# Linear attention's output product from f16 halves on two column groups of TensorE, and the output weights' forms made in one pass

## Chip, cores and metric

The kernel runs on one core of a Trainium2 chip. The metric is the device time of one execution in microseconds. A profile of one execution comes with it; its span runs from the first instruction to the last and is a little shorter than the device time.

The engines are named as in the profile: PE is TensorE's matrix multiplication and PEld its loading of weights, DVE is VectorE, ACT is ScalarE, POOL is GpSimd, and SP is SyncE, which here issues all transfers.

## What is computed

Two attention layers on separate inputs of 2048 tokens by 1024 features, 32 heads of 32 each, are computed and put side by side in a result of 2048 by 2048. Layer A is a softmax attention within four segments of 512 tokens with a compressive memory that is carried from segment to segment. Layer B is a linear attention with learned features, and the change lies in its second half and in A's output weights:

```python
q, k, v = qkv[0], qkv[1], qkv[2]
pq = jnp.einsum("bhsd,hdf->bhsf", q, w_phi)
pk = jnp.einsum("bhsd,hdf->bhsf", k, w_phi)
phi_q = jnp.concatenate([_softmax(pq, axis=-1), _softmax(-pq, axis=-1)], axis=-1)
phi_k = jnp.concatenate([_softmax(pk, axis=-1), _softmax(-pk, axis=-1)], axis=-1)
kv = jnp.einsum("bhsf,bhsd->bhfd", phi_k, v)
z  = jnp.einsum("bhsf->bhf", phi_k)
num = jnp.einsum("bhqf,bhfd->bhqd", phi_q, kv)
den = jnp.einsum("bhqf,bhf->bhq", phi_q, z)[..., None] + 1e-6
o = num / den
```

The result of each layer is then multiplied by its output weights `wo`, a matrix of 1024 by 1024.

## The kernel before

The inputs are f32, and most products are made from f16 halves. A number is scaled and split into a high half and a low half (what the high half left over); a product is then three matmuls, high by high, high by low and low by high, which add up in one bank of PSUM. `halves` (L377) does the split on ACT (high, L387) and DVE (low, L389); `split` (L345) does the same with f32r parts, a form of f32 that TensorE multiplies in one pass (L347 on ACT, L350 on DVE). `product` (L353, its matmuls at L360) runs the three matmuls over the depth. `strassen` (L544, matmuls at L552) computes a product of 2 by 2 blocks with seven block products; the sums of blocks that this needs are called forms, and `forms` (L451) makes them by a plan of steps (`XPLAN`, `WPLAN`): a subtraction of blocks on POOL (L459), then the halves. In its other mode, which takes blocks that are scaled already, the high half is a plain ACT copy (L466) and the low half a POOL subtraction (L467).

The program has four stages. First comes layer A's attention, head group by head group; layer B's weights are prepared beside it. Then come B's keys and values, eight pairs of row blocks of 128 tokens (L1217): projections by `strassen`, features by `expo` (L1102: maximum and minimum, two differences, the exponential on ACT, the sums r at L1125 and their reciprocal at L1128), the scaling on POOL (L1229), halves of the features (L1259, L1262), and the matmuls of features with values (L1269). DVE adds their results to `kva`, 64 by 64 numbers for each pair of heads of which only the two diagonal 32 by 32 blocks count; an addition for each half of the columns multiplies with `svm`, a scale made at L505 that is zero outside the own block (L1278 and L1281). The lower halves of the values are made at L1155, and Strassen's sums on DVE at L562. The keys' sums go to `za`.

The third stage is B's queries and output, 16 row blocks (L1387), and here the change lies. For each of two halves of the heads: features from `expo` (tile `e`, 16 heads by 64 features, five buffers); POOL multiplies them with the keys' sums `zb` into a tile `ez` that has one buffer, in two parts (L1418); DVE sums that to the denominators (L1420 to L1428); POOL scales `e` with the result (L1430). Then in two quarters, each for four pairs of heads: four transposes on PE (L1436); `split` to f32r parts `pt` (L347, L350); twelve matmuls with the keys' and values' sums `kls` as weights (L1446), 64 output rows for a pair of heads; and the eviction to the f16 halves `ot` by `halves`, for the first and the second pairs' outputs apart (L387, L389 on tiles of 64 rows by 256). A batch below means the twelve matmuls of one quarter; there are 16 x 2 x 2 = 64. `project` (L1318) multiplies `ot` with B's output weights (L360, output `misc`) and ACT scales the result (L1323). Between the row blocks, `weights` (L1357) makes the halves of A's output weights' seven forms: four blocks of columns, each read twice, three forms on the first reading and four on the second, subtractions on POOL (L1371), halves on ACT and DVE. The fourth stage is A's output product (L1459 on), by Strassen's method, with matmuls at L1498.

The order of the work is written by a planner, `Graph.run` (L148). Every `op` has an engine, an assumed duration and a priority, in most cases the number of its row block; the planner walks through time and gives each engine the ready operation of the lowest priority. What comes out is a fixed order for each engine, in which the engine then works, one instruction behind the other. So a changed duration or dependency changes the order of other work too. PSUM has eight banks, and the kind `pv`, into which the product goes, may hold one of them at a time (L77).

## Time and profile before

| what | value |
|---|---|
| median of 3 runs | 1818.51 us (1817.17 to 1818.78) |
| the profiled execution: device time | 1821.83 us |
| its span | 1819.5 us |
| instructions | 39261 |
| mean granted TensorE clock | 0.987 |
| bytes read and written in HBM | 149.64 and 85.00 MB |

In a row of the groups stand the line, the engine, the operation, what it writes and reads (buffer numbers left out), shapes, the count, the busy time in us with the mean ns of one, and the idle time of the engine before them with what ended it. A matmul's mean is its whole length; matmuls are pipelined, so the time that one takes from PE is the step from its start to the next one's start. In a row of waits stand who waited, for whom, the sum in us, how often, and the longest. In the order of time a row is a start, a length, an engine with its instruction, and how many were merged.

### The profile page before, as it was taken

To read this page: it belongs to the slowest core of one execution; us is meant where nothing else is said; L and a number is where in the kernel's file an instruction comes from. 1 tells how busy PE (TensorE), PEld (TensorE's weight loads), DVE (VectorE), ACT (ScalarE), POOL (GpSimd) and SP (SyncE) were. 2 spreads that over 40 slices of the span, in tenths; PEclk is the share of its full clock that TensorE was granted. 3 is DMA by queue.
4 is the path that set the end of the run, shared out by engine and by line. 5 is a ranking of instruction groups with operands and counts; after the bars stand their busy time and mean duration, and the time that the engine had idled before them with its cause. 6 is when DMAs were issued, how large, how long until landed. Compare 5 with 4: busy or idle time off the path is not lost. (4 is left out here: it accounts for less than half of the span.)

```text
span 1819.5 us, 39261 instructions
## 1 busy us (share of the span) xinstructions
PE 1747.2 (96%) x14712; PEld 1072.7 (59%) x14712; DVE 1503.4 (83%) x3523; ACT 1172.2 (64%) x2185; POOL 903.3 (50%) x1117
## 2 busy tenths in 40 slices
PE   8999998999999999999989999998999999999999
PEld 5767676677677766777544444444555555555444
DVE  6989989898777887888878999979998889887541
ACT  6896986877777877688756565546655455545341
POOL 6445454555757677678654444534444545431000
PEclk8999999999999999999989999999999999999999
DMA  6546554574545454574484343275323224334321
GB/s 202 168 141 197 138 173 137 170 216 148 149 115 146 132 171 124 164 213 118 141 274 144 139 156 134 89 265 222 111 64 104 83 88 133 109 130 128 111 74 64
DMA packets 174414, 263.13 MB, mean 145 GB/s; under 512 B 70032, under 2 KB 123024, under 8 KB 165520
## 3 DMA queue, kind: packets, MB, share of 16 engines
q1 hardware_dynamic: 174224, 260.63, 45.4%
q8 instruction: 115, 1.88, 0.4%
q14 instruction: 75, 0.61, 0.1%
HBM read 149.64 MB, written 85.00 MB: 129 GB/s over the span
## 5 line engine op out<-in xcount | busy, mean ns | idle before, releaser
L360 PE MATMUL proj<-S,S 128*128 128x128 f16 (+1 forms) x3072 | 504.0, 300 | 5.3 <-ACT S L387 3.3
L360 PEld LDWEIGHTS <-S 128*128 128x128 f16 x4608 | 331.8, 99 | 154.5 <-issue 10.6
L552 PE MATMUL proj<-S,S 128*128 128x512 f16 x1488 | 351.3, 384 | 10.8 <-ACT S L466 3.2
L552 PEld LDWEIGHTS <-S 128*128 128x128 f16 x1968 | 188.5, 99 | 229.7 <-issue 16.4
L883 POOL TENSOR_SCALAR_AFFINE_SELECT ph<-ph 128x256 f16<-128x256 f16 (+1 forms) x448 | 197.0, 462 | 172.9 <-DVE ph L877 136.2
L877 DVE SCALAR_TENSOR_TENSOR ph<-s,ph 128x512 f16<-128x512 f32 x320 | 210.6, 684 | 57.3 <-ACT ph L876 55.3
L778 DVE CUSTOM_DVE_ANT_0 s<-s,causal 128x512 f32<-128x512 f32 (+3 forms) x512 | 242.5, 511 | 11.8 <-PE s L772 8.2
L874 ACT ACTIVATE s<-s,bd 128x512 f32<-128x512 f32 x320 | 212.2, 707 | 22.6 <-PE s L870 22.1
L876 ACT ACTIVATE ph<-s 128x512 f16<-128x512 f32 x320 | 189.7, 651 | 1.1 <-PE pv L906 0.6
L360 PE MATMUL misc<-S,ot 128*128 128x512 f16 x768 | 180.5, 382 | 0.0
L1122 ACT ACTIVATE e<-e,sk 128x256 f32<-128x256 f32 x256 | 115.2, 501 | 72.3 <-DVE e L1119 68.2
L1418 POOL TENSOR_TENSOR ez<-e,zb 128x512 f32<-128x512 f32 x64 | 86.3, 1348 | 137.8 <-DVE dn L1420 82.5
L772 PE MATMUL s<-S 96*128 96x512 f16 (+3 forms) x512 | 113.3, 300 | 5.8 <-DVE mt L778 4.2
L870 PE MATMUL s<-S 104*128 104x512 f16 (+3 forms) x512 | 114.6, 302 | 1.8 <-DVE quad L1014 1.1
L360 PEld LDWEIGHTS <-ot 128*128 128x128 f16 x768 | 71.3, 98 | 74.6 <-issue 1.1
L360 PE MATMUL proj<-wv,S 128*128 128x128 f16 x1536 | 104.2, 221 | 0.3 <-DVE mt L778 0.3
L1229 POOL TENSOR_TENSOR e<-e,r 128x1024 f32<-128x1024 f32 x32 | 64.4, 2019 | 75.9 <-DVE r L1128 60.0
L906 PEld LDWEIGHTS <-ph 128*128 128x128 f16 x2560 | 87.8, 96 | 18.2 <-issue 2.5
L906 PE MATMUL pv<-vl,ph 128*128 128x66 f16 (+1 forms) x2560 | 92.7, 185 | 2.1 <-POOL ph L883 1.3
L387 ACT ACTIVATE ot<-pv,osc 64x256 f16<-64x256 f32 x128 | 59.9, 468 | 50.4 <-PE pv L1446 49.4
L1430 POOL TENSOR_TENSOR e<-e,r 128x1024 f32<-128x1024 f32 x32 | 65.4, 2043 | 44.3 <-DVE r L1428 43.7
L1125 DVE TENSOR_REDUCE r<-e 128x32 f32<-128x1024 f32 x64 | 77.0, 1209 | 10.2 <-ACT e L1122 10.1
(298 smaller groups left out, 3498.4 us busy)
## 6 DMA issues: line engine op xcount, KB each, us to landing
S<-h SPq DMA_DIRECT2D x192, 128.0 KB
S<-wf_d SPq DMA_DIRECT2D x21, 1024.0 KB
st<-bwqk SPq DMA_DIRECT2D x64, 256.0 KB
wf_d<-fo SPq DMA_DIRECT2D x48, 256.0 KB
h<-awo SPq DMA_DIRECT2D x24, 512.0 KB
out<-os SPq DMA_DIRECT2D x40, 256.0 KB
wf_d<-oT SPq DMA_DIRECT2D x36, 256.0 KB
S<-xf_d SPq DMA_DIRECT2D x9, 1024.0 KB
```

The lines of the kernel that those rows point to most:

```text
L360: op(PE, dur, lambda c=c, a=a, b=b, lv=lv, rv=rv: nc.tensor.matmul(pv(), lv(), rv(), start=(c == 0 and a + b == 0), stop=(c == n - 1 and a ...
L552: op(PE, 0.215, lambda n=n, a=a, b=b, lv=lv, rv=rv: nc.tensor.matmul(ps(), lv(), rv(), start=(start and n == 0 and a + b == 0), stop=(n == ...
L772: nc.tensor.matmul(ps()[:, o:o + 128 * i + 128], st()[0:96, 0, h, 128 * i:128 * i + 128], st()[0:96, 1, h, 0:128 * i + 128], start=True, s ...
L778: dve(0.12 + 0.00113 * n, lambda h=h, i=i, o=o, n=n: nc.vector.tensor_tensor_reduce(ps()[:, o:o + n], ps()[:, o:o + n], causal[:, 512 - n: ...
L870: nc.tensor.matmul(ps()[:, o:o + n], st()[0:104, 1, h, 128 * j:128 * j + 128], st()[0:104, 0, h, 128 * j:512], start=True, stop=True)
L874: act(0.59, lambda: nc.scalar.activation(ps(), ps(), AF.Exp, bias=0.0, scale=bd()[:, 4, i2, 0:1]), r=[(bd, i2)], w=[ps])
L876: act(0.5, lambda: nc.scalar.activation(ph()[:, 0], ps(), AF.Copy, scale=2.0 ** 14), r=[ps], w=[(ph, 0)])
L877: dve(0.6, lambda: nc.vector.scalar_tensor_tensor(ph()[:, 1], ps(), 2.0 ** 14, ph()[:, 0], op0=OP.mult, op1=OP.subtract), r=[ps, (ph, 0)], ...
L883: nc.gpsimd.affine_select(pd, pd, pattern=[[0, n], [1, 128]], compare_op=OP.is_ge, fill=0.0, base=0, channel_multiplier=-1)
L906: nc.tensor.matmul(ps()[:, i, n0:n1], ph()[:, a, o:o + 128], vl()[:, j, h, n0:n1], start=(i == 0 and a == 0), stop=(j == min(i, 2)), skip_ ...
L1122: op(ACT, 0.41, lambda i=i: nc.scalar.activation(e()[:, 4 * i:4 * i + 4], e()[:, 4 * i:4 * i + 4], AF.Exp, bias=0.0, scale=sk()[:, i:i + 1 ...
L1418: op(POOL, 1.2, lambda a=a, h0=h0, e=e, ez=ez: nc.gpsimd.tensor_tensor(ez(), e()[:, 8 * a:8 * a + 8], zv()[:, h0:h0 + 8], op=OP.mult), r=[ ...
```

## The change

Five things are changed.

1. The product of L1446 is made from f16 halves. `kls` is divided by the keys' sums (`zr`, the reciprocal of `za`, and by the largest scale), which bounds it, and masked to the diagonal blocks at the same time (`zs`), once per half of the heads; its halves are made by ACT and DVE. `pt` becomes f16 halves with a factor 2^14. The features have been multiplied with the keys' sums, so that the product is the same.
2. The twelve matmuls become one operation for the planner. Even pairs of heads go to PSUM rows 0 to 63 and odd pairs to rows 64 to 127, in turn, which uses the first 64 and the last 64 columns of the array. The output is then 128 rows by 256 columns, and one ACT and one DVE instruction evict it.
3. POOL writes the features times the keys' sums over the features (no `ez`); it must wait for r, which is summed from the features, and the scaling of L1430 then applies to the product.
4. In the keys' stage one addition over 64 columns per pair replaces the two that masked, and `svm` goes.
5. `weights` reads each block of columns once, scales both parts in place on ACT, and makes all seven forms with `forms` in the mode that uses POOL for the low halves. The transfers of A's output weights fall from 24 to 16.

```diff
--- before.py
+++ after.py
-        op(DVE, 0.1, lambda: nc.vector.tensor_scalar(svm[:, p], bm2, pst[:, p, 0:1], 1.0 / EUP, op0=OP.mult, op1=OP.mult),
-           r=[(pstb, (p, 0))], w=[(svmb, p)], prio=prio)
...
                     else:
                         nc.vector.scalar_tensor_tensor(o, i, s, o, op0=OP.mult, op1=OP.add)
 
-                for two in range(2):
-                    op(DVE, 0.2, lambda add=add, hb=hb, j=j, two=two, kv=kv, p=p: add(
-                        kva[hb]()[:, 4 * j:4 * j + 4, 32 * two:32 * two + 32], kv()[:, :, 32 * two:32 * two + 32],
-                        svm[:, p, two:two + 1]), r=[kv, (svmb, p)], w=[(kva[hb], (j, two))], prio=P)
+                op(DVE, 0.34, lambda add=add, hb=hb, j=j, kv=kv, p=p: add(
+                    kva[hb]()[:, 4 * j:4 * j + 4], kv()[:, :, 0:64], pst[:, p, 0:1]),
+                   r=[kv, (pstb, (p, 0))], w=[(kva[hb], j)], prio=P)
                 op(DVE, 0.08, lambda add=add, hb=hb, j=j, kv=kv: add(
-                    za()[:, 8 * hb + 4 * j:8 * hb + 4 * j + 4], kv()[:, :, 64], 1.0 / EUP), r=[kv], w=[(za, (hb, j))], prio=P)
+                    za()[:, 8 * hb + 4 * j:8 * hb + 4 * j + 4], kv()[:, :, 64], 1.0), r=[kv], w=[(za, (hb, j))], prio=P)
         x = xn if p + 1 < NT // 2 else None
 
...
-            zb()[:, 4 * q:4 * q + 4, :].rearrange("p a b -> p (a b)"), ps(), AF.Copy), r=[ps], w=[(zb, q)], prio=P)
-    kls = G.buf("b", [128, 2, NG, 2, 64], F32R, "kls")
-    for q in range(4):
-        hl = [(kls, (a, q), lambda a=a, q=q: kls()[:, a, 2 * q:2 * q + 2].rearrange("p g b d -> p (g b) d")) for a in range(2)]
-        src = (kva[q // 2], lambda q=q: kva[q // 2]()[:, 4 * (q % 2):4 * (q % 2) + 4].rearrange("p g d -> p (g d)"))
-        split(*hl, src, 256, P)
-
+            zb()[:, 4 * q:4 * q + 4, :].rearrange("p a b -> p (a b)"), ps(), AF.Copy, scale=1.0 / EUP), r=[ps], w=[(zb, q)], prio=P)
-       r=[(bigs, 1)], w=[(oscs, 1)], prio=P)
-    op(DVE, 0.12, lambda: nc.vector.reciprocal(osc2[:, 1, 1:2], osc2[:, 1, 0:1]), w=[(oscs, 1)], prio=P)
+       r=[(bigs, 1)], w=[(oscs, 1)], prio=P - 5)
+    op(DVE, 0.12, lambda: nc.vector.reciprocal(osc2[:, 1, 1:2], osc2[:, 1, 0:1]), w=[(oscs, 1)], prio=P - 5)
+    kls = G.buf("b", [128, 2, 16, 64], F16, "kls")
+    for hb in range(2):
+        zr, zs, v = G.buf("b", [128, 8], F32, "zr", 2), G.buf("b", [128, 8, 2], F32, "zs", 2), slice(8 * hb, 8 * hb + 8)
+        op(DVE, 0.1, lambda zr=zr, v=v: nc.vector.tensor_scalar(zr(), za()[:, v], 1e-12, None, op0=OP.max),
+           r=[(za, (hb, 0)), (za, (hb, 1))], w=[zr], prio=P)
+        op(DVE, 0.12, lambda zr=zr: nc.vector.reciprocal(zr(), zr()), w=[zr], prio=P)
+        op(DVE, 0.1, lambda zr=zr: nc.vector.tensor_scalar(zr(), zr(), osc2[:, 1, 1:2], 2.0, op0=OP.mult, op1=OP.mult),
+           r=[(oscs, 1)], w=[zr], prio=P)
+        op(DVE, 0.1, lambda zr=zr, zs=zs: nc.vector.tensor_tensor(
+            zs(), zr()[:, :, None].to_broadcast([128, 8, 2]), bm2[:, None, :].to_broadcast([128, 8, 2]), op=OP.mult),
+           r=[zr], w=[zs], prio=P)
+        op(DVE, 0.62, lambda zs=zs, hb=hb: nc.vector.tensor_tensor(
+            kva[hb]().rearrange("p g (b d) -> p g b d", d=32), kva[hb]().rearrange("p g (b d) -> p g b d", d=32),
+            zs()[:, :, :, None].to_broadcast([128, 8, 2, 32]), op=OP.mult), r=[zs], w=[kva[hb]], prio=P, port=True)
+        op(ACT, 0.53, lambda hb=hb, v=v: nc.scalar.activation(kls()[:, 0, v], kva[hb](), AF.Copy),
+           r=[kva[hb]], w=[(kls, (0, hb))], prio=P)
+        op(DVE, 0.62, lambda hb=hb, v=v: nc.vector.tensor_tensor(kls()[:, 1, v], kva[hb](), kls()[:, 0, v], op=OP.subtract),
+           r=[kva[hb], (kls, (0, hb))], w=[(kls, (1, hb))], prio=P, port=True)
...
-    def weights(j, second, prio):
+    def weights(j, prio):
         t = blocks(j, prio)
-        some = ((3, "B22"), ((1, 0), 0, None), ((3, 1), 1, "T3"), ((3, 0), 3, "T2"), ((2, 3), 2, "T4")) if second else (
-            (0, "B11"), (2, "B21"), ((1, 0), 0, "T1"))
...
-                op(POOL, 1.28, lambda pv=pv, av=av, bv=bv: nc.gpsimd.tensor_tensor(pv(), av(), bv(), op=OP.subtract),
...
-                halves(*hl, (pb, pk, pv), (wscs, (2, 0), lambda: wsc[:, 2, 0]), 512, prio)
...
+        for k in range(2):
+            op(ACT, 1.05, lambda k=k: nc.scalar.activation(t[k](), t[k](), AF.Copy, scale=wsc[:, 2, 0, 1:2]),
+               r=[(wscs, (2, 0))], w=[(t[k], 0), (t[k], 1)], prio=prio)
+
+        def dst(f):
+            n = ("B11", "B21", "T2", "T1", "T3", "B22", "T4")[f]
+            if n in wform:
+                return *((wform[n], (a, j), lambda a=a: wform[n]()[:, a, j, :]) for a in range(2)), lambda: None
+            o, i = G.buf("b", [128, 2, 512], F16, "cs", 4), SECOND.index(n)
+            return *((o, a, lambda a=a: o()[:, a]) for a in range(2)), lambda: op(
+                SP, 0.6, lambda: nc.sync.dma_start(wo_d[i, :, :, j, :], o()), r=[o], w=[(wob, i)], prio=prio, lat=1.5, kb=256)
+
+        forms(WPLAN, lambda k: (t[k // 2], k % 2, lambda: t[k // 2]()[:, k % 2]), dst, None, prio, POOL)
...
-        if 5 <= c < 13:
-            weights((c - 5) % 4, c >= 9, P + 0.5)
+        if c in (5, 7, 9, 11):
+            weights((c - 5) // 2, P + 0.5)
...
-                ez = G.buf("b", [128, 8, 2, 32], F32, "ez", 1)
-                op(POOL, 1.2, lambda a=a, h0=h0, e=e, ez=ez: nc.gpsimd.tensor_tensor(
-                    ez(), e()[:, 8 * a:8 * a + 8], zv()[:, h0:h0 + 8], op=OP.mult), r=[e, zb], w=[ez], prio=P)
-                op(DVE, 0.6, lambda a=a, ez=ez, dn=dn: nc.vector.tensor_reduce(
-                    dn()[:, 8 * a:8 * a + 8], ez(), axis=AX.X, op=OP.add), r=[ez], w=[(dn, a)], prio=P)
+                op(POOL, 1.35, lambda a=a, h0=h0, e=e: nc.gpsimd.tensor_tensor(
+                    e()[:, 8 * a:8 * a + 8], e()[:, 8 * a:8 * a + 8], zv()[:, h0:h0 + 8], op=OP.mult),
+                   r=[zb, r], w=[(e, ("x", a))], prio=P)
+                op(DVE, 0.66, lambda a=a, e=e, dn=dn: nc.vector.tensor_reduce(
+                    dn()[:, 8 * a:8 * a + 8], e()[:, 8 * a:8 * a + 8], axis=AX.X, op=OP.add), r=[(e, ("x", a))], w=[(dn, a)], prio=P)
...
-                pt = G.buf("b", [128, 2, 4, 128], F32R, "pt", 3)
+                pt = G.buf("b", [128, 2, 4, 128], F16, "pt", 3)
-                split((pt, 0, lambda pt=pt: pt()[:, 0]), (pt, 1, lambda pt=pt: pt()[:, 1]), (ps, ps), 512, P)
-                pn = bank("pv", [64, 2, 2, 128])
+                op(ACT, 0.55, lambda pt=pt, ps=ps: nc.scalar.activation(pt()[:, 0], ps(), AF.Copy, scale=2.0 ** 14),
+                   r=[ps], w=[(pt, 0)], prio=P)
+                op(DVE, 0.62, lambda pt=pt, ps=ps: nc.vector.scalar_tensor_tensor(
+                    pt()[:, 1], ps(), 2.0 ** 14, pt()[:, 0], op0=OP.mult, op1=OP.subtract), r=[ps, (pt, 0)], w=[(pt, 1)], prio=P)
+                pn = bank("pv", [128, 2, 128])
-                for i in range(4):
-                    def v(pn=pn, i=i):
-                        return pn()[:, i % 2, i // 2, :]
-
-                    for a, b in ((0, 0), (0, 1), (1, 0)):
-                        op(PE, 0.056, lambda a=a, b=b, v=v, i=i, pt=pt, p0=p0: nc.tensor.matmul(
-                            v(), kls()[:, a, (p0 + i) // 2, i % 2, :], pt()[:, b, i, :], start=(a + b == 0), stop=(a == 1)),
-                           r=[(kls, (a, (p0 + i) // 4)), (pt, b)], w=[pn], prio=P)
-                for b in range(2):
-                    hl = [(ot, (a, b, hb, q), lambda a=a, b=b, p0=p0, otv=otv: otv()[
-                        64 * b:64 * b + 64, a, p0 // 2:p0 // 2 + 2, :]) for a in range(2)]
-                    halves(*hl, (pn, lambda b=b, pn=pn: pn()[:, b]), (oscs, 1, lambda: osc2[0:64, 1]), 256, P, port=False)
+
+                def f(pn=pn, pt=pt, p0=p0):
+                    for g in range(2):
+                        for a, b in ((0, 0), (0, 1), (1, 0)):
+                            for k in range(2):
+                                nc.tensor.matmul(pn()[64 * k:64 * k + 64, g, :], kls()[:, a, p0 + 2 * g + k, :], pt()[:, b, 2 * g + k, :],
+                                                 start=(a + b == 0), stop=(a == 1), skip_group_check=True)
+
+                op(PE, 0.5, f, r=[(kls, (0, hb)), (kls, (1, hb)), pt], w=[pn], prio=P)
+                op(ACT, 0.33, lambda pn=pn, p0=p0, otv=otv: nc.scalar.activation(
+                    otv()[:, 0, p0 // 2:p0 // 2 + 2, :], pn(), AF.Copy, scale=2.0 ** -15), r=[pn], w=[(ot, (0, hb, q))], prio=P)
+                op(DVE, 0.35, lambda pn=pn, p0=p0, otv=otv: nc.vector.scalar_tensor_tensor(
+                    otv()[:, 1, p0 // 2:p0 // 2 + 2, :], pn(), 2.0 ** -15, otv()[:, 0, p0 // 2:p0 // 2 + 2, :], op0=OP.mult, op1=OP.subtract),
+                   r=[pn, (ot, (0, hb, q))], w=[(ot, (1, hb, q))], prio=P)
```

The next rows are from PE's order at the start of the third stage, the first quarter of the first row block. Before, `pv<-pt,kls` is the product, `proj` a matmul of the next pair's queries:

```order
L552 LDWEIGHTS S_19265
L552 MATMUL proj<-S_18973,S_19265 128x512
L371 MATMUL s<-ast,one 128x1
L1446 MATMUL pv<-pt,kls 64x128 x11
L552 LDWEIGHTS S_19548
L552 MATMUL proj<-S_18379,S_19548 128x512
```

The first of the twelve, which needs the high half alone, stands ten rows further up, and the other eleven here. After, the same place for the second quarter:

```order
L549 LDWEIGHTS S_19509
L549 MATMUL proj<-S_18350,S_19509 128x512
L1434 MATMUL s<-ident,e 128x128 x3
L1447 LDWEIGHTS kls
L1447 MATMUL pv<-pt,kls 64x128
```

The twelve now stand together, each with its load of weights as an instruction of its own, behind both halves of the features; here they stand between the transposes of the next half (`s<-ident,e`).

The second place is POOL's order where the output weights are made. Before, `h` are the blocks of weights:

```order
L1418 TENSOR_TENSOR ez<-e,zb 128x512
L1371 TENSOR_TENSOR h_21072<-h_21072 128x512
L1418 TENSOR_TENSOR ez<-e,zb 128x512
L1371 TENSOR_TENSOR h_21072<-h_21077,h_21072 128x512
L1418 TENSOR_TENSOR ez<-e,zb 128x512
L1430 TENSOR_TENSOR e<-e,r 128x1024
```

After, `S` and `cs` are the low halves of forms (L466 is the former L467, L458 the former L459, L1428 the former L1430):

```order
L1428 TENSOR_TENSOR e<-e,r 128x1024 x3
L466 TENSOR_TENSOR S_20599<-h_19490,S_20599 128x512
L466 TENSOR_TENSOR S_20608<-h_19521,S_20608 128x512
L466 TENSOR_TENSOR cs<-h_19521,cs 128x512
L458 TENSOR_TENSOR h_19490<-h_19490 128x512
L458 TENSOR_TENSOR h_19490<-h_19521,h_19490 128x512
L466 TENSOR_TENSOR S_20646<-h_19490,S_20646 128x512
L458 TENSOR_TENSOR h_19521<-h_19521,h_19490 128x512
L466 TENSOR_TENSOR cs<-h_19490,cs 128x512
L458 TENSOR_TENSOR h_19521<-h_19521 128x512
L466 TENSOR_TENSOR cs<-h_19521,cs 128x512 x2
L466 TENSOR_TENSOR S_20599<-h_20732,S_20599 128x512
```

The weights' work no longer alternates with the features' but stands in longer runs, twelve instructions in this one, between two scalings of features.

22 lines of the change are left out of this document (2 added, 20 removed).

## The prediction

> **What bounds the kernel now.** I read the page first, then the busy time of the engines stage by stage, then TensorE's waits in two stages, then the order of time around the product that is changed.
>
> ```profile
> PE 1747.2 (96%) x14712; PEld 1072.7 (59%) x14712; DVE 1503.4 (83%) x3523; ACT 1172.2 (64%) x2185; POOL 903.3 (50%) x1117
> ```
>
> TensorE is busy for 96% of the span, but that is a mean over stages. The three stages that matter here are the keys of the linear attention (955 to 1280 us), its queries and output (1280 to 1660 us) and the other attention's output projection (1660 to the end); the last is not touched. The columns are the stretch, its length, then the busy time of PE, PEld, DVE, ACT and POOL.
>
> ```profile
> 955.00:1280.00 325.00, 302.39 (x2043) 150.87 (x2042) 299.28 (x538) 185.07 (x383) 144.23 (x102) 0.99 0.46 163
> 1280.00:1660.00 380.00, 363.61 (x2317) 205.46 (x2316) 337.62 (x626) 200.97 (x406) 178.20 (x121) 0.99 0.32 105
> ```
>
> In the query stage PE is busy for 363.6 of 380 us and stands still for 16.4. DVE is second with 337.6 us (89%). POOL and ACT are at about half. So a microsecond off PE's own work comes off the span there, as long as DVE and the chains through POOL keep up; a microsecond off DVE alone only takes away part of PE's standing. These are what PE waits for, first in the query stage, then in the key stage:
>
> ```profile
> PE s L1436 <- POOL e L1430: 9.0, 13, 2.6
> PE pv L1446 <- DVE pt L350: 5.8, 4, 2.3
> ```
>
> ```profile
> PE kv L1269 <- DVE pt L1262: 4.8, 8, 1.3
> PE kv L1269 <- DVE ot L1155: 4.4, 4, 2.6
> PE kv L1269 <- ACT pt L1259: 3.2, 1, 3.2
> PE proj L552 <- DVE cs L562: 2.4, 2, 1.6
> ```
>
> In the query stage 9.0 us end with the feature tile that POOL scales (L1430) and 5.8 us with the lower half that DVE makes (L350). In the key stage PE stands for 22.6 us in all, and 11.6 us of the quoted waits end with DVE.
>
> **The product itself.** This is what it costs PE, from PE's order of time in the query stage (start, length, instruction, count), and from the chain of waits a plain run of the big products:
>
> ```profile
> 1362.31 1.07 PE L1446 MATMUL pv<-pt,kls 128*64 128x128 f32 x12
> 1363.22 2.33 PE L360 MATMUL misc<-S,ot 128*128 128x512 f16 x10
> 1365.21 1.01 PE L1446 MATMUL pv<-pt,kls 128*64 128x128 f32 x11
> ```
>
> ```profile
> 1660.96 10.36 PE misc L360 x48
> ```
>
> A matmul of 512 columns takes 10.36 / 48 = 0.216 us of PE's time. From one batch's start to the next are 2.90 us, of which ten big matmuls take 2.16; the twelve small ones take 0.74 us, 62 ns each. There are 64 batches (16 row blocks, two halves, two quarters), so the product holds PE for 64 x 0.74 = 47 us. The changed product has as many matmuls, of the same 128 moving columns and 64 output rows, but each pair of heads alternates between the first and the last 64 columns of the array. Nothing in this trace runs on the last 64 alone, so the cost is bounded from both sides. If the two groups run beside each other, two matmuls go in the time of one: 0.37 us per batch, a gain of 0.37 x 64 = 23.7 us. If they run one after the other, the nearest row is the f16 matmul of 128 columns:
>
> ```profile
> 310.82 1.56 PE L360 MATMUL proj<-wv,S 128*128 128x128 f16 x25
> ```
>
> ```profile
> L360 PE MATMUL proj<-wv,S 128*128 128x128 f16 x1536 | 104.2, 221 | 0.3 <-DVE mt L778 0.3
> L1446 PEld LDWEIGHTS pv<-pt,kls 128*64 128x64 f32 x768 | 57.8, 138 | 22.8 <-DVE pt L350 8.9 <-ACT pt L347 1.6 <-issue 0.5
> L798 PEld LDWEIGHTS <-mh 128*8 128x8 f16 x128 | 6.5, 85 | 7.9 <-issue 3.6 <-DVE mh L793 1.2 <-DVE mt L778 0.4
> ```
>
> Twenty-five of them in 1.56 us, the last with its 0.22 us of length, make 24 steps of 56 ns. Twelve take 0.67 us and the gain is only 0.07 x 64 = 4.5 us. What speaks for this end is the weight load: 64 columns take 138 ns and 8 columns 85 ns, so a column costs (138 - 85) / 56 = 0.95 ns and 64 of them 61 ns, which is just the step of 62 ns. If loads of the two groups go one behind the other, the groups gain nothing. What speaks for the other end is that a load already goes beside a running matmul here (a step of 62 ns holds a load of 61 and a matmul of 56), and that the two groups have weights and output rows of their own. I take the first end, 23.7 us, with a chance a little over a half, since nothing that the two groups share shows as a limit in a row except the load.
>
> The Trainium skill, in "TensorE: Matmul & The Clock Gate", section "Why this matters for your kernels", says that small outputs on separate column groups run beside each other, and gives 2.38 times for three groups of 32 with 512 moving columns; by that the first end holds, and no run here shows it yet. Against it stands "TensorEngine Tiling (Array Packing)", Restrictions: column tiling switches the fast weight load off; with the other page's rule that a load takes its columns divided by 1.2 in ns, an estimate is 53 ns for 64 columns, 0.64 us per batch and a gain of 6.4 us.
>
> **DVE and ACT in the query stage.** The eviction of the product, the weights' halves and one row for scale:
>
> ```profile
> L389 DVE SCALAR_TENSOR_TENSOR ot<-pv,osc,ot 64x256 f16<-64x256 f32 x128 | 60.3, 471 | 8.4 <-ACT ot L387 6.7
> L387 ACT ACTIVATE ot<-pv,osc 64x256 f16<-64x256 f32 x128 | 59.9, 468 | 50.4 <-PE pv L1446 49.4
> L389 DVE SCALAR_TENSOR_TENSOR cs<-h,wsc,cs 128x512 f16<-128x512 f32 x16 | 13.4, 844 | 0.3 <-ACT cs L387 0.3
> L389 DVE SCALAR_TENSOR_TENSOR S<-h,wsc,S 128x512 f16<-128x512 f32 x12 | 10.2, 854 | 1.7 <-ACT S L387 1.6
> L467 POOL TENSOR_TENSOR fo<-S,fo 128x512 f16<-128x512 f32 x16 | 18.9, 1184 | 6.0 <-ACT fo L466 6.0
> L1371 POOL TENSOR_TENSOR h<-h 128x512 f32<-128x512 f32 x12 | 15.8, 1316 | 7.3 <-DVE S L389 7.0
> L832 DVE TENSOR_TENSOR amem<-misc,dm 128x256 f32<-128x256 f32 x48 | 20.1, 421 | 1.0
> ```
>
> Each batch's four evictions on 64 rows become two on 128 rows and as many columns. L832 does 256 columns of PSUM on 128 rows in 421 ns, so twice the rows cost no more, and DVE and ACT each lose half: 64 x 0.47 = 30 us. The weights' 28 lower halves (13.4 + 10.2 = 23.6 us) go from DVE to POOL; at 1.18 us each they cost POOL 28 x 1.18 = 33 us, less four subtractions of 1.32 (5 us), since the blocks are read and combined once and not twice. The keys' sums add a dozen DVE instructions once, about 3 us, at the start of the stage, where PE has the first pair's big products to run. The first half of the features gains a factor on ACT, which is under half loaded. DVE falls to 338 - 30 - 24 + 3 = 287 us, POOL rises to 178 + 33 - 5 = 206. None of this sets the end; it shortens what PE waits for. DVE falls by 15%, and I take the same 15% of PE's 16.4 us: 2.4 us, with ends at 0 and 8 (half of the standing).
>
> **The features times the keys' sums** (L1418) are now written over the features, so they wait for the sum r over the features, and no longer for a single spare buffer:
>
> ```profile
> POOL ez L1418 <- DVE dn L1420: 82.5, 29, 16.2
> L1418 POOL TENSOR_TENSOR ez<-e,zb 128x512 f32<-128x512 f32 x64 | 86.3, 1348 | 137.8 <-DVE dn L1420 82.5 <-ACT e L1122 22.5 <-DVE mx L1115 22.2
> L1125 DVE TENSOR_REDUCE r<-e 128x32 f32<-128x1024 f32 x64 | 77.0, 1209 | 10.2 <-ACT e L1122 10.1
> ```
>
> The wait of 82.5 us for the buffer goes; in its place each tile waits 1.2 us for r. Behind it on POOL stand the scaling of the features (L1430) and now the weights' halves, and PE's transposes wait for the former. I cost it at nothing, as five feature tiles are in flight; 32 x 1.2 = 38 us of latency is what it could cost without that cover, and it is part of the rival on POOL below.
>
> **The key stage.** DVE adds up the products of keys and values in one instruction of 256 columns for two of 128, and the scales' table goes:
>
> ```profile
> L1278 DVE SCALAR_TENSOR_TENSOR kva<-kv,svm,kva 128x128 f32<-128x128 f32 x28 | 8.4, 343 | 1.4 <-PE kv L1269 1.4
> L1278 DVE SCALAR_TENSOR_TENSOR ez<-kv,svm,ez 128x128 f32<-128x128 f32 x28 | 8.3, 338 | 4.0 <-PE kv L1269 4.0
> L505 DVE TENSOR_SCALAR svm<-bm,pst 128x2 f32<-128x2 f32 x5 | 2.7, 537 | 0.0
> L877 DVE SCALAR_TENSOR_TENSOR ph<-s,ph 128x512 f16<-128x512 f32 x320 | 210.6, 684 | 57.3 <-ACT ph L876 55.3
> ```
>
> Between 128 columns at 0.34 us and 512 at 0.68, 256 come to 0.455: 32 x 0.455 = 14.6 us for 64 x 0.34 = 21.8, and with the scales 2.7 us more, DVE loses 9.9 us of 299. PE is 93% busy there, so at most 9.9 and at least nothing comes off the span. DVE ends about half of PE's waits, and part of each cut only moves PE's wait to the next thing; I take a third, 3 us.
>
> **Sum.** 23.7 + 2.4 + 3 = 29.1 us. The profiled execution took 1821.8 us for a span of 1819.5, 3.3 over the median of the runs, 1818.5; I take the cut off the median: 1818.5 - 29.1 = 1789.4, rounded 1789.5 us.
>
> **Rivals.** *The groups take turns* (35%): the product gains 4.5 us, the rest stays: 4.5 + 2.4 + 3 = 9.9 us, 1808.6 us. For it: the load's 61 ns fill the step. Against it: the loads go to different columns. In this case the change doesn't do what it says for PE, and DVE's relief is all there is.
>
> *POOL becomes what PE waits for* (12%), slower. Place: POOL's queue where the output weights are made; the order shows twelve of their instructions one behind the other there. POOL takes instructions in order; PE's transposes wait for L1430 already, 9.0 us in 13 waits. Price: if PE stands for each of the 28 new halves, 33 us; with the groups taking turns that ends at 1818.5 - 9.9 + 33 = 1841.6 us, and at 1822 with both groups at work. It decides from 9.9 us (29.1 with both groups) of new standing. Against it: POOL at 206 us is little over half loaded, and PE has the big products of the next pair of blocks to run meanwhile.
>
> *No more than the middle*: the groups overlap in part, 42 ns a step, 0.5 us a batch: 15 us from the product and 1798 us. It is part of the likeliest case.
>
> **Numbers.** Both groups at work 53%, taking turns 35%, POOL 12%. The low end of the range is the first case with 7 us from the key stage and 2 more of PE's standing: 1783. The high end is the second with the product's 4.5 us alone: 1814. It leaves out POOL's 12% and some tenth of the others. A measurement of this kernel tells 0.2%, 3.6 us, from no change. Faster: all of the first case and six in seven of the second, 0.83. Within: the rest of the second and a sixth of the third, 0.07. Slower: 0.10.
>
> **What would show it.** Right: the product's twelve matmuls in 0.37 us of PE's order of time, in pairs that start together; query stage near 354 us; DVE near 287 us in it; no new wait of PE over 10 us. Wrong: steps of 56 ns or more between the matmuls (the groups take turns), transposes that wait for L1430's successor for more than 20 us (POOL), or a key stage that moves by more than 8 us in either direction, which would mean that the new order itself, not these prices, decides there.

## The result, and the profile after

| what | before | after |
|---|---|---|
| median, in runs on the same chip | 1818.64 us (1817.17 to 1818.78) | 1788.62 us (1787.82 to 1790.01) |
| span of the profiled execution | 1819.5 us | 1788.1 us |
| instructions | 39261 | 39000 |

The ratio is 0.9838, with a 95% interval of 0.982 to 0.9855. The change takes off 30.0 us; the forecast was 29.1 and 1789.5 us. The sum was right, two of its terms were not, and they nearly cancel. First the page's line of the engines, of after, and then the busy time of PE, PEld, DVE, ACT and POOL in the key stage and in the query stage, which ends some 20 us earlier now:

```profile
PE 1723.7 (96%) x14712; PEld 1039.1 (58%) x14712; DVE 1445.7 (81%) x3399; ACT 1135.9 (64%) x2127; POOL 915.8 (51%) x1141
```

```profile
955.00:1280.00 325.00, 301.55 (x2042) 151.42 (x2041) 299.04 (x509) 184.80 (x384) 143.28 (x105) 0.98 0.44 160
1280.00:1640.00 360.00, 352.65 (x2357) 177.75 (x2356) 289.50 (x546) 172.70 (x358) 192.62 (x142) 1.00 0.30 102
```

In the query stage PE stands still for 360 - 352.65 = 7.3 us where it stood for 16.4. DVE is at 289.5 us. In the key stage DVE is busy for 299.04 us, as before (299.28), and PE for 301.55 (302.39). That stretch is fixed in time, and the stage begins earlier after; between the two cuts that are described below, DVE is busy for 357.6 us before and 354.8 after. PE's waits in the query stage, with the wait of POOL that took the place of the one for the spare tile, and then PE's in the key stage:

```profile
POOL e L1415 <- DVE r L1122: 67.6, 12, 12.9
...
PE s L1434 <- POOL e L1428: 4.4, 4, 1.8
...
PE pv L1447 <- DVE pt L1438: 1.6, 3, 0.7
```

```profile
PE kv L1266 <- DVE ot L1152: 7.3, 6, 2.6
...
PE proj L549 <- ACT cs L555: 3.9, 5, 1.5
PE kv L1266 <- DMA S<-xf_d: 3.9, 1, 3.9
```

PE's two waits in the query stage have fallen from 9.0 to 4.4 and from 5.8 to 1.6 us. In the key stage the waits have changed their names more than their sum. POOL waits for r instead of the buffer, 67.6 us for 82.5, and PE's wait for the scaling behind it on POOL has become shorter, not longer.

Now the product in PE's order of time, then the loads of one batch on PEld:

```profile
1383.56 1.24 PE L359 MATMUL misc<-S,ot 128*128 128x512 f16 x5
1384.73 0.53 PE L1447 MATMUL pv<-pt,kls 128*64 128x128 f16 x12
1385.19 1.25 PE L359 MATMUL misc<-S,ot 128*128 128x512 f16 x5
1386.37 0.53 PE L1447 MATMUL pv<-pt,kls 128*64 128x128 f16 x12
```

```profile
1384.73 0.36 PEld L1447 LDWEIGHTS <-kls 128*64 128x64 f16 x12 [0.42 <-issue]
```

From one batch to the next are 1.64 us, of which five big matmuls take 5 x 0.216 = 1.08; the twelve take 0.56 us. That is neither the 0.37 of two groups beside each other nor the 0.67 of turns. The single records of this batch tell why. The two matmuls of a pair start 3 or 4 ns apart, the second pair starts 80 ns after the first, and from then on a new pair follows every 56 ns: the groups do run beside each other, and twelve starts span 0.31 us. But the last big matmul starts at 1384.423 and the first of the twelve at 1384.732: 309 ns, 93 more than a big matmul's step of 216. From the last start of the twelve to the next big matmul are 152 ns instead of a step of 56. Over all batches that stand between big matmuls the medians are the same, 309 and 152 ns. So each batch pays some 0.19 us (93 + 152 - 56) on the way in and out; with the first pair's longer step (80 for 56) it is 0.21 us. The row of PEld shows the first half of it: the load begins with the batch, after 0.42 us in which PEld waits for nothing that the profile shows. Before, the same row looked like this, and the load began while the big matmuls ran:

```profile
1362.28 0.95 PEld L1446 LDWEIGHTS pv<-pt,kls 128*64 128x64 f32 x12
```

The product's matmul began at 1362.31 there, 0.03 us behind its load. These are the groups of after that have a price in the forecast:

```profile
L1447 PE MATMUL pv<-pt,kls 128*64 128x128 f16 x768 | 34.0, 223 | 1.6 <-DVE pt L1438 1.6
L1453 DVE SCALAR_TENSOR_TENSOR ot<-pv,ot 128x256 f16<-128x256 f32 x64 | 26.4, 414 | 16.3 <-ACT ot L1451 16.2
L1451 ACT ACTIVATE ot<-pv 128x256 f16<-128x256 f32 x64 | 24.3, 380 | 50.1 <-PE pv L1447 49.8
L466 POOL TENSOR_TENSOR cs<-h,cs 128x512 f16<-128x512 f32 x16 | 18.5, 1160 | 8.9 <-ACT cs L465 8.9
L466 POOL TENSOR_TENSOR S<-h,S 128x512 f16<-128x512 f32 x12 | 14.6, 1222 | 10.5 <-ACT S L465 10.5
L1275 DVE SCALAR_TENSOR_TENSOR kva<-kv,pst,kva 128x256 f32<-128x256 f32 x14 | 6.6, 474 | 1.4 <-PE kv L1266 1.4
```

The evictions take 26.4 us of DVE and 24.3 of ACT, for 60.3 and 59.9; the weights' halves take 33.1 us of POOL (33 were forecast); an addition of 256 columns takes 474 ns (455).

**Where the 31.4 us of the spans are.** I cut each execution at two points in PE's records: the first matmul of the keys' and values' projections, and the last of L1269 (after: L1266). Up to the first is unchanged work: 876.7 us before, 873.5 after; that is scatter (experiment 11, with the instructions of before, took 872.9). The key stage took 400.9 us and takes 401.4. All that follows took 542.0 and takes 513.2: 28.8 us. In these, the batches' own time on PE (from the end of the last big matmul's step to the start of the next, without waits), summed over all 64, went from 49.5 to 35.9 us, 13.6 us; PE's standing gives 9.0 more. The big matmuls of the query stage took 2.9 us more than 216 ns each before, mostly right behind the three longest waits, and take 0.6 now: 2.3 us. About 4 us I can't lay on single records, whose ends are modelled.

### The profile page after: what moved, and what is told of

It reads as the page before. It is cut to its first block, busy times and chain, and to the rows that moved or that the text cites. A ratio compares the mean times of both kernels' runs of the same rounds, so it can differ in the third digit from the quotient of the medians.

```text
span 1788.1 us, 39000 instructions
## 1 busy us (share of the span) xinstructions
PE 1723.7 (96%) x14712; PEld 1039.1 (58%) x14712; DVE 1445.7 (81%) x3399; ACT 1135.9 (64%) x2127; POOL 915.8 (51%) x1141
## 4 chain that ended last, share of the span: by engine, by line
PE 59%; DVE 23%; ACT 3%; issue 2%; POOL 1%; DMA 0%; ACTq 0%; DVEq 0%; POOLq 0%
PE proj L359 19%; PE proj L549 9%; PE misc L359 7%; PE proj L1501 5%; PE pv L903 3%; PE s L867 3%; PE s L769 2%; PE s L1501 2%; DVE s L775 2%; DVE S L388 2%; DVE r L1122 2%; DVE mx L1112 2%; DVE e L1116 1%; PE pv L1447 1%; PE misc L1501 1%
## 5 line engine op out<-in xcount | busy, mean ns | idle before, releaser
L871 ACT ACTIVATE s<-s,bd 128x512 f32<-128x512 f32 x320 | 212.0, 708 | 20.9 <-PE s L867 20.5
L1119 ACT ACTIVATE e<-e,sk 128x256 f32<-128x256 f32 x256 | 113.4, 498 | 82.5 <-DVE e L1116 79.2
L1415 POOL TENSOR_TENSOR e<-e,zb 128x512 f32<-128x512 f32 x64 | 81.2, 1292 | 74.4 <-DVE r L1122 67.6
L1226 POOL TENSOR_TENSOR e<-e,r 128x1024 f32<-128x1024 f32 x32 | 64.4, 2016 | 61.3 <-DVE r L1125 50.4
L1428 POOL TENSOR_TENSOR e<-e,r 128x1024 f32<-128x1024 f32 x32 | 61.8, 1935 | 49.9 <-DVE r L1426 49.3
L549 PE MATMUL s<-S,S 128*128 128x512 f16 x324 | 77.1, 379 | 1.8 <-ACT cs L555 1.8
```

The source lines that it names most:

```text
L549: op(PE, 0.215, lambda n=n, a=a, b=b, lv=lv, rv=rv: nc.tensor.matmul(ps(), lv(), rv(), start=(start and n == 0 and a + b == 0), stop=(n == ...
L871: act(0.59, lambda: nc.scalar.activation(ps(), ps(), AF.Exp, bias=0.0, scale=bd()[:, 4, i2, 0:1]), r=[(bd, i2)], w=[ps])
L1119: op(ACT, 0.41, lambda i=i: nc.scalar.activation(e()[:, 4 * i:4 * i + 4], e()[:, 4 * i:4 * i + 4], AF.Exp, bias=0.0, scale=sk()[:, i:i + 1 ...
```

## The experiments

The theory: the two groups run beside each other; what the product gains less than forecast goes into the stall at each batch's ends; and the rest comes from PE's waits. The rivals: the groups take turns and the gain is elsewhere; one of the other parts brings it; and the new order of the work, not the prices of its parts, decides. Every ratio is to the kernel before, run beside it on the same chip; differences to the changed kernel are ratio differences times 1818.5 us. A ratio's interval is about 0.0015 to each side, so such a difference is uncertain by some 4 us. The table has one profiled execution of each: key stage and rest by the two cuts above, the batches' own time on PE, and the median of one batch (for the sixth, of 24 matmuls).

| kernel | median us | ratio | key stage | rest | batches | one batch |
|---|---|---|---|---|---|---|
| before | 1818.64 | 1 | 400.9 | 542.0 | 49.5 | 0.726 |
| after | 1788.62 | 0.9838 (0.982 to 0.9855) | 401.4 | 513.2 | 35.9 | 0.551 |
| 1 six and six | 1794.50 | 0.9869 (0.9854 to 0.9884) | 399.6 | 519.1 | 44.3 | 0.690 |
| 2 one group | 1809.40 | 0.9953 (0.9936 to 0.9969) | 399.9 | 532.5 | 57.5 | 0.883 |
| 3 weights as before | 1793.96 | 0.9865 (0.985 to 0.988) | 399.7 | 517.9 | 37.0 | 0.552 |
| 4 spare tile | 1794.40 | 0.9869 (0.9854 to 0.9884) | 401.0 | 516.7 | 37.3 | 0.552 |
| 5 two additions | 1796.22 | 0.9869 (0.9855 to 0.9884) | 402.9 | 514.1 | 35.7 | 0.552 |
| 6 batches of 24 | 1786.82 | 0.9818 (0.9803 to 0.9833) | 398.4 | 511.6 | 30.1 | 0.886 |
| 7 all columns | 1798.60 | 0.9887 (0.9871 to 0.9904) | 399.7 | 523.9 | 44.4 | 0.670 |
| 8 four evictions | 1797.75 | 0.9879 (0.9864 to 0.9893) | 400.0 | 522.4 | 38.2 | 0.552 |
| 9 planner 0.55 | 1788.43 | 0.9836 (0.9821 to 0.9851) | 398.9 | 514.7 | 36.6 | 0.552 |
| 10 planner 0.68 | 1793.42 | 0.9863 (0.9845 to 0.9881) | 399.6 | 519.0 | 37.5 | 0.552 |
| 11 before, planner 0.06 | 1815.85 | 0.9981 (0.9971 to 0.999) | 402.0 | 539.8 | - | - |
| 12 product alone | 1801.17 | 0.9907 (0.989 to 0.9923) | 402.8 | 519.4 | 36.2 | 0.552 |

### 1. Six matmuls of one group, then six of the other

```diff
-                    for g in range(2):
-                        for a, b in ((0, 0), (0, 1), (1, 0)):
-                            for k in range(2):
+                    for k in range(2):
+                        for g in range(2):
+                            for a, b in ((0, 0), (0, 1), (1, 0)):
```

> The changed kernel, with the twelve matmuls of a batch in another order: the six of the first column group, then the six of the second; everything else as it is. Theory (the groups run beside each other, and this gave about 14 us; the other 13 came from shorter waits of PE): neighbours now share a group, so the steps go from pairs every 52 ns to single steps of 52 to 60 ns, a batch from 0.56 to about 0.87 us, and the time rises by 64 x 0.3 = 19 us to about 1808 us. Rival (the groups give nothing, relief of DVE and POOL is all): 1789 us, same.

The order of time on PE:

```profile
1384.01 0.66 PE L1447 MATMUL pv<-pt,kls 128*64 128x128 f16 x12
1384.61 1.25 PE L359 MATMUL misc<-S,ot 128*128 128x512 f16 x5
1385.79 0.66 PE L1447 MATMUL pv<-pt,kls 128*64 128x128 f16 x12
```

It cost 5.6 us. A batch takes 1.78 - 1.08 = 0.70 us, with the same 309 and 152 ns at its ends. That is between the two outcomes I had thought of: in the single records twelve starts still take 0.45 us and not 0.6, with steps of 5 to 56 ns behind the first one of 80, so the second group's matmuls start while the first's six run. Writing the groups apart did not make them take turns, and so this run alone did not say what the groups are worth.

### 2. All twelve on the first 64 columns

```diff
-                pn = bank("pv", [128, 2, 128])
+                pn = bank("pv", [64, 2, 2, 128])
...
-                                nc.tensor.matmul(pn()[64 * k:64 * k + 64, g, :], kls()[:, a, p0 + 2 * g + k, :], pt()[:, b, 2 * g + k, :],
+                                nc.tensor.matmul(pn()[:, k, g, :], kls()[:, a, p0 + 2 * g + k, :], pt()[:, b, 2 * g + k, :],
```

The eviction becomes two of 64 rows each on ACT and on DVE, as before. The sums of two pairs of heads begin in turn in the same rows of one bank here, and the result lacks a part of them; the instructions are as many.

> The changed kernel, with all f16 matmuls on the first column group as before the change (64 rows by 512 columns of output, alternating between the pairs of heads) and so four evictions on 64 rows instead of two. Theory: steps of 56 ns, 0.67 us a batch without the stall at its ends and 0.87 with it, and DVE gets 26 us of evictions back: 64 x 0.11 to 0.31 = 7 to 20 us plus about 5 of waits, 1801 to 1814 us. Rival (groups give nothing): only the evictions, 1789 to 1794 us. It also tells where the new stall of 0.09 us ahead of each batch is from: if from the f16 load of 64 columns, the first load still waits here; if from the second group, the first load starts beside the last big matmul, as it did with f32r.

```profile
1402.94 0.86 PE L1447 MATMUL pv<-pt,kls 128*64 128x128 f16 x12
1403.73 1.47 PE L359 MATMUL misc<-S,ot 128*128 128x512 f16 x6
1405.13 0.86 PE L1447 MATMUL pv<-pt,kls 128*64 128x128 f16 x12
```

A batch takes 2.19 - 6 x 0.216 = 0.89 us, in steps of 56 ns. The second group is worth 0.883 - 0.551 = 0.33 us a batch, 21 us in all, and the kernel is 20.9 us slower than the changed one. The four evictions are in this difference too, and in experiment 8 they cost 7.5 us by themselves. Here PE stands for 5.3 us behind the key stage, not 7.3, so its order of time shows no price for them. The rival of turns has fallen. On one group the f16 product is slower than the f32r product of before, 0.883 us a batch for 0.726: without the second group, the f16 halves would have cost PE time. The ends of a batch are the same, 309 and 152 ns, so the stall doesn't come from the second group.

### 3, 4 and 5. One of the other parts undone

In 3 `weights` is that of before, with two readings of each block and the lower halves on DVE:

```diff
-    def weights(j, prio):
+    def weights(j, second, prio):
...
-        forms(WPLAN, lambda k: (t[k // 2], k % 2, lambda: t[k // 2]()[:, k % 2]), dst, None, prio, POOL)
...
+                halves(*hl, (pb, pk, pv), (wscs, (2, 0), lambda: wsc[:, 2, 0]), 512, prio)
```

In 4 the spare tile `ez` is back; the product there leaves out the multiplication by the keys' sums:

```diff
+                ez = G.buf("b", [128, 8, 2, 32], F32, "ez", 1)
...
-                    e()[:, 8 * a:8 * a + 8], e()[:, 8 * a:8 * a + 8], zv()[:, h0:h0 + 8], op=OP.mult),
-                   r=[zb, r], w=[(e, ("x", a))], prio=P)
+                    ez(), e()[:, 8 * a:8 * a + 8], zv()[:, h0:h0 + 8], op=OP.mult), r=[e, zb], w=[ez], prio=P)
```

In 5 there are two additions again:

```diff
-                op(DVE, 0.34, lambda add=add, hb=hb, j=j, kv=kv, p=p: add(
-                    kva[hb]()[:, 4 * j:4 * j + 4], kv()[:, :, 0:64], pst[:, p, 0:1]),
-                   r=[kv, (pstb, (p, 0))], w=[(kva[hb], j)], prio=P)
+                for two in range(2):
+                    op(DVE, 0.2, lambda add=add, hb=hb, j=j, two=two, kv=kv, p=p: add(
+                        kva[hb]()[:, 4 * j:4 * j + 4, 32 * two:32 * two + 32], kv()[:, :, 32 * two:32 * two + 32],
+                        pst[:, p, 0:1]), r=[kv, (pstb, (p, 0))], w=[(kva[hb], (j, two))], prio=P)
```

> The changed kernel with the output weights' halves made as before: two readings, low halves on DVE, subtractions on POOL. DVE gets 24 us back, POOL loses 28. Theory (relief of DVE is what shortened PE's waits, some 24 of 54 us of it from here): 4 to 7 us slower, 1793 to 1796 us. Rival (PE's waits shrank because of POOL's single spare buffer, not of DVE): same, 1788 to 1790 us; if POOL's new load costs something, a little faster.

> The changed kernel with the features times the keys' sums in a tile of their own again, one buffer, as before; the product then leaves out the multiplication by the keys' sums. Theory that the single buffer held POOL and so PE's transposes: 3 to 6 us slower, 1792 to 1795 us. Rival (DVE's relief alone): 1788 to 1790 us; if the wait for r costs more than the buffer did, up to 3 us faster.

> The changed kernel with the sums of keys and values added in two instructions of 32 columns per pair again, without the mask. DVE gets about 6 us back in the key stage. Theory of the prediction (a third of DVE's cut there comes off the span): 2 us slower, 1790 to 1791 us. Rival (the key stage did not move between the two profiles, 401 us from its first product to its last sums, so this part is worth nothing): 1788 to 1789 us.

They cost 4.9, 5.6 and 5.6 us; the last is more than either outcome that I had named for it. By these alone each part would carry about a sixth of the gain. Experiments 9 to 11 show why that may not be said.

### 6. Batches of 24

```diff
-                pn = bank("pv", [128, 2, 128])
...
+            def f(pn=pn, pts=pts, p0=p0):
+                for g in range(4):
+                    for a, b in ((0, 0), (0, 1), (1, 0)):
+                        for k in range(2):
```

The two quarters of a half share a bank of PSUM and one operation, so there are 32 batches with half as many ends, and half as many evictions of twice the columns.

> The changed kernel with both quarters' matmuls in one batch of 24, one bank, and one ACT and one DVE eviction of 512 columns. Theory (each entry to and exit from the small matmuls costs PE a stall of about 0.2 us, whatever the batch's size): 32 stalls fewer, 32 x 0.2 = 6 us, and DVE and ACT lose 32 x 0.15 us each, so 1781 to 1783 us unless PE waits longer for the later of the two halves. Rival (the stall grows with the batch, or what is saved goes into waits for the later quarter): 1788 us or slower.

```profile
1384.75 2.32 PE L359 MATMUL misc<-S,ot 128*128 128x512 f16 x10
1387.00 0.86 PE L1448 MATMUL pv<-pt,kls 128*64 128x128 f16 x24
1387.79 2.12 PE L359 MATMUL misc<-S,ot 128*128 128x512 f16 x9
```

24 matmuls take 3.04 - 2.16 = 0.88 us. Against two batches of 0.551 that saves 0.216 us, about one pair of ends with the first pair's longer step. The batches' own time falls by 5.8 us. PE's wait for the scaled features grows from 4.4 to 7.0 us; that the product now needs both quarters may be the reason, which no run shows by itself:

```profile
PE s L1436 <- POOL e L1428: 7.0, 9, 1.4
```

It is the fastest kernel of the study, at 1786.82 us. By the ratios it is 3.6 us ahead of the changed kernel, less than the theory's 6 to 8, and the intervals overlap.

### 7. The same product over all 128 columns

```diff
-    kls = G.buf("b", [128, 2, 16, 64], F16, "kls")
+    kls = G.buf("b", [128, 2, 16, 128], F16, "kls")
...
-                                nc.tensor.matmul(pn()[64 * k:64 * k + 64, g, :], kls()[:, a, p0 + 2 * g + k, :], pt()[:, b, 2 * g + k, :],
-                                                 start=(a + b == 0), stop=(a == 1), skip_group_check=True)
+                                nc.tensor.matmul(pn()[:, g, :], kls()[:, a, p0 + 2 * g + k, :], pt()[:, b, 2 * g + k, :],
+                                                 start=(a + b + k == 0), stop=(a + k == 2), skip_group_check=True)
```

The weights of an even pair of heads stand in the first 64 columns and zeros in the others, those of an odd pair the other way round; all twelve then use the whole array, one after the other.

> The changed kernel with weights of 128 columns: a pair's 64 columns stand in the half that its output rows take, zeros in the other, so that twelve matmuls of the full array add up in the same 128 rows and nothing runs on a part of the array. Theory that the stall at both ends of a batch is a change of the array's mode between whole and half width: no stall, twelve steps of 56 ns, 0.67 us a batch instead of 0.55: 64 x 0.12 = 8 us slower, 1796 us. Rival (the stall comes from f16 weights of this small product being new and late, or from anything else than the mode): 0.67 + 0.19 us a batch, 20 us slower, 1808 us.

First PE's order of time, then PEld's loads of the middle batch:

```profile
1390.14 0.83 PE L1455 MATMUL pv<-pt,kls 128*128 128x128 f16 x12
1390.81 1.24 PE L359 MATMUL misc<-S,ot 128*128 128x512 f16 x5
1391.88 0.83 PE L1455 MATMUL pv<-pt,kls 128*128 128x128 f16 x12
```

```profile
1389.92 0.87 PEld L1455 LDWEIGHTS <-kls 128*128 128x128 f16 x12
```

A batch takes 0.67 us: twelve steps of 56 ns and nothing else. The stall is gone at both ends (the medians are the plain steps, 216 ns in and 56 out, where there were 309 and 152), and the load begins 0.22 us ahead of its matmul, beside the last big one. Against experiment 2, with as many matmuls one after the other, a batch is 0.883 - 0.670 = 0.213 us shorter. So the stall belongs to the change between instructions on 64 columns and on 128, and not to the batch, its loads' number or its dependencies. Whether it is the narrow load or the narrow matmul that PE stops for, the run doesn't tell, since both are wide here. As the two groups save more than the stall costs, the kernel is 8.9 us slower than the changed one, and the batches' own time is 8.5 us longer.

### 8. Four evictions of 64 rows

```diff
+                for k in range(2):
+                    op(ACT, 0.33, lambda pn=pn, p0=p0, otv=otv, k=k: nc.scalar.activation(
+                        otv()[64 * k:64 * k + 64, 0, p0 // 2:p0 // 2 + 2, :], pn()[64 * k:64 * k + 64], AF.Copy, scale=2.0 ** -15), r=[pn], w=[(ot, (0, hb, q, k))], prio=P)
```

DVE's instruction is doubled in the same way.

> The changed kernel with the product's output evicted in four instructions on 64 rows instead of two on 128; nothing else. DVE and ACT get about 26 us each back. Theory that relief of DVE shortened PE's waits: 4 to 7 us slower, 1793 to 1796 us. Rival (the evictions are beside the path, and only the weights and the spare tile count): 1788 to 1790 us.

```profile
L1454 DVE SCALAR_TENSOR_TENSOR ot<-pv,ot 64x256 f16<-64x256 f32 x128 | 53.6, 419 | 10.7 <-ACT ot L1452 9.1
L1452 ACT ACTIVATE ot<-pv 64x256 f16<-64x256 f32 x128 | 48.2, 376 | 49.1 <-PE pv L1447 48.0
```

64 rows cost as much as 128 (419 and 376 ns for 414 and 380), so DVE has 27 us more to do. The kernel is 7.5 us slower; the changed kernel's waits of PE for DVE's halves grow:

```profile
PE pv L1447 <- DVE pt L1438: 5.7, 9, 2.2
```

### 9, 10 and 11. Only a number of the planner

```diff
-                op(PE, 0.5, f, r=[(kls, (0, hb)), (kls, (1, hb)), pt], w=[pn], prio=P)
+                op(PE, 0.55, f, r=[(kls, (0, hb)), (kls, (1, hb)), pt], w=[pn], prio=P)
```

```diff
-                op(DVE, 0.66, lambda a=a, e=e, dn=dn: nc.vector.tensor_reduce(
+                op(DVE, 0.68, lambda a=a, e=e, dn=dn: nc.vector.tensor_reduce(
```

```diff
-                        op(PE, 0.056, lambda a=a, b=b, v=v, i=i, pt=pt, p0=p0: nc.tensor.matmul(
+                        op(PE, 0.06, lambda a=a, b=b, v=v, i=i, pt=pt, p0=p0: nc.tensor.matmul(
```

In 10 the sum of L1418 is planned at 0.68 instead of 0.66, and in 11 the kernel before plans its small matmuls (L1446) at 0.06 instead of 0.056. The instructions are the same; only the order in which the planner puts them differs.

> The changed kernel with one number of the planner changed: a batch is assumed to take 0.55 us (which is what it takes) instead of 0.5. No instruction is added or removed, only the order moves. It measures what another order alone is worth. If the 5 to 8 us that each undone part cost are these parts' own worth: 1787 to 1790 us. If they are what any new order costs beside a lucky one: 1792 to 1797 us.

> The changed kernel with another number of the planner changed: DVE's sums of the denominators are assumed to take 0.68 us instead of 0.66. Again only the order moves. Same two outcomes: 1787 to 1790 us if the parts have a worth of their own, 1792 to 1797 us if any new order costs.

> The kernel before with one number of the planner changed: each of the product's matmuls is assumed to take 0.06 us (as measured) instead of 0.056. Only the order moves. It tells whether the kernel before stood in an order that was luckier or unluckier than others: 1816 to 1821 us if the order is worth little, 1812 or 1825 us if it is worth as much as a part of the change.

The first changes nothing (0.4 us faster by the ratios). The second is 4.5 us slower, and the third is 3.5 us faster than the kernel before, with an interval of 0.9971 to 0.999. The third is clear of the noise; the second's 4.5 us are hardly more than the 4 us by which such a difference is uncertain. The second's profile is of its slowest execution (1797.77 us), and there one row stands out: PE waits for DVE's halves of the features for 7.5 us, which was 1.6.

```profile
PE pv L1447 <- DVE pt L1438: 7.5, 7, 2.4
```

So a new order alone can move this kernel by about 4 us, nearly as much as each of experiments 3, 4 and 5 did. What one of these parts brings stays open. Only the product (20.9 us between one group and two) is far above it, and the evictions' 7.5 lie just above.

### 12. The product and its evictions alone

Experiments 3, 4 and 5 in one kernel: weights as before, the spare tile, two additions. It too leaves out the multiplication by the keys' sums.

> The changed kernel with three parts undone at once: the output weights as before, the spare tile for features times keys' sums (the product then leaves out that multiplication), and two additions per pair in the key stage. What is left of the change are the f16 halves, the two groups and the two evictions. Theory (PE's own 13.6 us of the product, some 5 of shorter waits through the evictions, the other parts 5 us each less what they share): 1799 to 1803 us. Rival (product and evictions are worth all, the parts' 5 us come from the order alone): 1793 to 1797 us.

It is 16.9 us faster than the kernel before (0.0093 x 1818.5) and 12.5 us slower than the changed one. The three other parts together are thus worth some 12.5 us (uncertain by 4), which is about three times what an order alone moved; the rival, that product and evictions are worth all, has fallen. The windows of its query stage, then PE's two waits there:

```profile
1280.00:1640.00 360.00, 350.04 (x2329) 174.66 (x2329) 321.32 (x572) 164.73 (x345) 179.26 (x121) 1.00 0.33 112
```

```profile
PE s L1445 <- POOL e L1439: 5.6, 7, 1.9
...
PE pv L1458 <- DVE pt L1449: 3.6, 3, 2.6
```

DVE is busy for 321 us of the same stretch in which the changed kernel needs 289.5, and PE stands for 10.0 us there, not 7.3.

## Why the forecast was right, point by point

*The product on PE* (forecast 23.7 us, measured 13.6): the mechanism was right and the size wrong. The chance "a little over a half" for two groups beside each other rested on "nothing that the two groups share shows as a limit in a row except the load". The groups do run so, and the loads go beside each other (experiments 1, 2 and the single records). What the step left out is that a batch has ends. The forecast took the price of a batch as twelve steps and nothing else, because the f32r batches of before, with the same 64 output rows, showed nothing else; the f16 batches on 64 columns pay 0.19 us each. 64 x 0.19 = 12 us is the gap between 23.7 and 13.6, and a little more, as the batches of before took 49.5 us and not the 47 that the forecast began from. The middle that I named (42 ns a step, 0.5 us a batch, 15 us) is closest in size, for a reason that I did not have.

The Trainium skill states the rule that was missing, in "TensorEngine Tiling (Array Packing)", section Tiling Modes, Key Properties: a change of the tiling mode, unlike a change of the tile, drains TensorE. It gives no figure. The trace agrees for f16: 0.19 us per batch between 64 and 128 columns, nothing within 128 columns (experiment 7), and 3 or 4 ns from one group to the other. It doesn't cover the f32r matmuls of before, which had 64 output rows and loads of 64 columns between big matmuls and show no stall (0.726 us for twelve, steps of 60 ns). Why is open; f32r on the second group was not tried.

*PE's standing in the query stage* (forecast 2.4, bounds 0 to 8; measured 9.0, and 2.3 of slower matmuls behind waits): too small, and out of its bounds. The step "DVE falls by 15%, and I take the same 15% of PE's 16.4 us" takes a wait as proportional to the busy time of its engine. Waits are what is left when an engine comes late. DVE went from 89% to 80% busy, and both of PE's waits, for POOL's scaling and for DVE's halves, fell by half or more. With DVE at 321 us (experiment 12) PE stands for 10.0. Some of it may also be order: experiment 10 was 4.5 us slower with the same instructions, at the edge of the noise.

*DVE and ACT* (forecast DVE 287, POOL 206): DVE 289.5, POOL 192.6; the evictions, the halves and the additions came at about their prices. POOL is lower for the most part because the features' two products on it took less than before (81.2 and 61.8 us for 86.3 and 65.4), which no term had. The forecast's "Each batch's four evictions on 64 rows become two on 128 rows" at no more cost is shown by experiment 8.

*The features times the keys' sums* (forecast nothing): the wait for r came, 67.6 us in 12 waits of POOL, and PE's wait for the scaling behind it fell. That the cover held is shown by the rows. Experiment 4, 5.6 us, cannot be told from an order's worth.

*The key stage* (forecast 3, bounds 0 to 9.9): 0.5 us longer in the two executions. That pair settles nothing. Over the ten kernels here with one addition the key stage takes 398.4 to 401.4 us, 399.8 on average; over the four with two (before, 5, 11 and 12) 400.9 to 402.9, 402.2 on average. The difference of 2.3 us is near the forecast, but one execution of each could not show it, since it scatters as much. DVE's busy time in the fixed stretch of 325 us says little of it, since the stage starts 3.2 us earlier after, so that the stretch cuts the two executions at different work. By their rows the additions and the scales' table took 22.7 us before and 15.0 after, but between the two cuts DVE came down by only 2.8 us, not by the 9.9 of the forecast; some of the product's new weights are made on DVE ahead of the second cut. So even if the stage became 2.3 us shorter, that a third of 9.9 us came off is not shown.

*The rivals.* The groups take turns (35%): they don't, by experiment 2. POOL becomes what PE waits for (12%): POOL is 54% busy (192.6 of 360), and PE's wait for it fell from 9.0 to 4.4 us. That a new order decides was named as what a move of the key stage would mean. It does not carry the 30 us, but it is as large as any of the small terms.

*The signs.* DVE near 287 us and no new wait of PE over 10 us came true. The twelve matmuls in 0.37 us did not (0.55), nor did a query stage that is shorter by 26 us (it is some 20).

So 29.1 us had 10 us too much in the product and 9 too little in PE's standing and the slow matmuls behind waits; some 4 us belong to no term. That the forecast lies 1 us from the result is luck; what its terms are worth is said above.

## What to carry to other kernels

Before putting small products on a part of TensorE's columns, count how often PE changes between part and whole, and price each change from a row where it happens. Larger batches have fewer changes: in experiment 6 they took 5.8 us off PE's own work, though the time gained was not clear of the noise. To learn what one part of a change is worth in a kernel whose order a planner writes, first move a planner's number by a few per cent: what that does to the time is the smallest effect that an experiment with one part undone can show. And price an engine's relief by the waits that end with it, with all of them as the upper end, and not by a share of its busy time.
